# Moving one pair of heads from the float32 path to the split-float32 path in a fused attention and MLP kernel

## The chip, the cores and the metric

The kernel runs on one core of one Trainium2 chip. The metric is device time in microseconds from one launch, median of the runs shown. TensorE (PE), VectorE (DVE), ScalarE (ACT), GpSimd (POOL) and the queue of SyncE (SP), which issues nearly all loads and stores, each take their instructions in a fixed order and meet through semaphores.

## The reference

```
q, k, v: [4, 8, 768, 64] float32;  n_sink = 4, window = 128
scores = q k^T / 8, kept where key < n_sink or 0 <= query - key < window, else -1e9
a = softmax(scores);  attn = a v
x = attn as [3072, 512]
h = x @ w_in            # [3072, 2048]
out = (h * sigmoid(h)) @ w_out   # [3072, 512]
```

## The kernel before

The 3072 tokens are handled in eight chunks of 384 (half a batch each, numbered c = 0 to 7). The eight heads of a chunk are four pairs, so there are 32 pairs p = 0 to 31; pairs 0 to 3 belong to chunk 0, 4 to 7 to chunk 1, and so on. A pair's attention gives 128 columns of x. The MLP of a chunk has sixteen steps fc = 0 to 15: twelve matmuls `h<-xh,winh` and the like (line 852, 128 hidden units by 384 tokens), SiLU twice on ACT (`gh`, rounded, and `sg`, line 863 and 864), their difference `gl` on DVE (line 866), and nine matmuls into `out` (lines 878 to 880). Every MLP operand is split into a rounded high part and a remainder, so three products stand for one float32 product. The two h banks in PSUM mean that step fc + 2 cannot start on PE before ACT has read step fc.

There are two ways through attention. **The float32 way** (`f_` functions) is used for pairs p < FP: q and k are transposed on PE (line 673), the scores are full float32 matmuls (line 720, two records each in the profile), the three query blocks are masked on DVE (line 727), exponentiated on ACT (line 742), turned into a reciprocal on DVE (lines 746 and 747), normalized on ACT (line 753), transposed on PE (lines 765 to 770), copied back by ACT and DVE (lines 771 to 776), and multiplied by v in float32 (line 788). **The split way** is used for p >= FP: DVE transposes q and k (lines 390, 410), ACT and DVE split them into parts, the scores are twelve one-pass matmuls (lines 464, 468), POOL normalizes (line 505) and splits by mask (lines 536, 540), and the product with v takes six matmuls of the `o<-pq,vs` kind a head and one for the sink keys (line 591). The split way needs the sink keys of all heads laid out beforehand (`ksA`, `ksB`); the function `sinks` does that once, with four small loads into `ksn`, four small transposes into `kst` (line 300), two copies on ACT and two subtractions on DVE.

The weights come as 32 blocks of 512 KB, eight for each of four groups g (four of w_in, four of w_out). A block is loaded into `wraw` (lines 802, 805), turned into float32 bits by three DVE instructions on `wcv` (lines 41 to 43), rounded on ACT (line 826) and its remainder taken on DVE (line 828; POOL for the first six). `wraw`, `ksn` and the output staging share one tag, `ost`, with two buffers in rotation, so a load waits until the block two places before it has been converted. I write raw1_0 for block 0 of group 1, r4_0 for the reciprocals of pair 4's first head, pa0_4 for its first transposed probabilities, s5_0 for the scores of pair 5's first head, o4 for pair 4's product with v, and gh0_0 for chunk 0, step 0.

All of this is written as closures with a due time T, in units of one MLP step, and emitted in the order of T. The table `OPT` gives the due times; the framework then sets each engine's order from that, taking what is ready and earlier due. The lines that matter:

```
        at(O["tk"], sinks)
            if p < FP:
                ...
                        z = O["s1"]
                        T = O["S"] + O["F1"] + (u - 2 * HP) * z
        for g in range(NG):
            for i in range(NCC + FG):
                at(O["w"][g] + O["wd"][g] * i, lambda g=g, i=i: weight(g, i))
```

Here u = 2p + j counts heads, HP is 4, `s1` is the spacing of the float32 heads of chunk 1, `tk` the due time of `sinks`, and `w`, `wd` are the start and the spacing of a weight group.

Of the kernel before, what the change touches and what calls it, by code (L numbers as in the profile page):

```python
# [25 lines left out]

OPT = dict(
    S=7.901, s0=0.903, f_l=2.468, f_p=-1.643, f_v=3.079, f_sm=0.693, f_pt=0.795, f_av=0.251,
    tk=15.973, s1=1.65, F1=1.024, D0=2.076, w=[0.458, 8.623, 11.237, 18.573], wd=[0.85, 0.58,
    1.293, 0.67], wc=19.252, wcd=2.681, warm=7, wg=4, ord=1, edge=8, dua=15, adp=0, glp=0,  # L30
    ptv=7, fill=[0, 4, 0, 0, 1, 0, 0, 2], na=[2, 16], lod=[6, 32], nv=[0, 0], hid=[0, 0],
    ktd=[0, 0], a=dict(load=-3.44, q=0.257, k=-0.012, v=1.813, s=1.461, sd=0.613, sm=1.795,
    smd=0.605, pt0=2.725, st=3.866, pt1=3.355, av0=4.289, av1=4.669), m0=dict(act=0.108,
    m2=1.206), m=dict(act=1.068, m2=1.546), fin=0.927, FP=8,
)


# [997 lines left out]
```

## Time and profile before

| what | value |
|---|---|
| median of 2 runs | 723.79 us (722.8 to 724.79) |
| the profiled execution | 723.66 us, its span 721.8 us |
| granted TensorE clock, mean | 0.998 |
| PE busy | 705.0 us of the span |
| DVE, ACT, POOL busy | 481.3, 489.4, 281.5 us |
| loaded and stored | 61.86 MB |

Matmuls overlap in their records, so the duration of one (346 ns for a 384-wide h matmul) is about twice the step from one start to the next (0.175 us in steady state). Costs of PE work below are therefore read from start to start.

### The profile page before, as it was taken

The numbers are of one execution on the slowest core, as the hardware profiler recorded it, in microseconds if no ns is written. First come the engines' busy times: TensorE is split into PE (matmuls) and PEld (weight loads), VectorE is DVE, ScalarE is ACT, GpSimd is POOL, SyncE is SP. The second block draws the span as 40 slices with busy tenths as digits, with TensorE's granted clock in tenths as the row PEclk, the third lists the DMA queues.
The fourth block names the chain that finished last, engine by engine and source line by source line (L and its number), as shares of the span: only waits on it lengthen the run. The fifth ranks groups of instructions, "written<-read, shape, count | busy, mean of one in ns | idle before, by whom it ended". The sixth has DMA issues, their size and how long they took to land.

```text
span 721.8 us, 12275 instructions
## 1 busy us (share of the span) xinstructions
PE 705.0 (98%) x3842; PEld 624.1 (86%) x3842; DVE 481.3 (67%) x1323; ACT 489.4 (68%) x1165; POOL 281.5 (39%) x667
## 2 busy tenths in 40 slices
PE   6998999999999999999999999999999999999997
PEld 4676778798999999999999999999999999998986
DVE  5899767976776687667866777767866776731111
ACT  4889788786776777777666777777667876732112
POOL 3310000055655666444555455544554554430000
PEclk9999999999999999999999999999999999999999
DMA  7556546434522262114521353114412321001001
GB/s 180 176 154 186 148 112 173 151 84 107 147 43 40 70 187 63 22 39 138 138 41 27 84 166 66 35 34 120 136 27 41 106 58 35 1 1 45 0 1 46
DMA packets 141334, 61.86 MB, mean 86 GB/s; under 512 B 130001, under 2 KB 130001, under 8 KB 141265
## 3 DMA queue, kind: packets, MB, share of 16 engines
q1 hardware_dynamic: 140976, 61.04, 32.9%
q8 instruction: 31, 0.51, 0.3%
q14 instruction: 39, 0.31, 0.1%
q10 hardware_dynamic: 288, 0.00, 0.0%
HBM read 54.72 MB, written 6.29 MB: 85 GB/s over the span
## 4 chain that ended last, share of the span: by engine, by line
PE 81%; DMA 5%; DVE 5%; ACT 3%; POOL 2%; issue 2%; SPq 1%; DVEq 0%; POOLq 0%; ACTq 0%
PE h L852 32%; PE out L880 11%; PE out L879 11%; PE out L878 11%; PE o L575 4%; DMA wraw<-in_moe_w_in_dram 3%; PE o L788 2%; PE s L468 2%; PE s L464 2%; PE pt L520 2%; DMA wraw<-in_moe_w_out_dram 2%; PE o L591 1%; DVE wcv L43 1%; DVE wcv L42 1%; PE o L584 1%
## 5 line engine op out<-in xcount | busy, mean ns | idle before, releaser
L852 PE MATMUL h<-xh,winh 128*128 128x384 f32 x512 | 177.2, 346 | 0.0
L852 PE MATMUL h<-xh,winl 128*128 128x384 f32 x512 | 173.9, 340 | 0.0
L852 PE MATMUL h<-xl,winh 128*128 128x384 f32 x512 | 172.7, 337 | 0.0
L878 PE MATMUL out<-wouth,gh 128*128 128x512 f32 x384 | 153.2, 401 | 1.7 <-ACT gh L863 1.6
L879 PE MATMUL out<-woutl,gh 128*128 128x512 f32 x384 | 151.8, 396 | 0.5 <-DVE woutl L828 0.3
L880 PE MATMUL out<-wouth,gl 128*128 128x512 f32 x384 | 150.2, 396 | 0.0
L863 ACT ACTIVATE gh<-h 128x384 fp32r<-128x384 f32 x128 | 62.9, 492 | 104.4 <-PE h L852 100.7
L866 DVE TENSOR_TENSOR gl<-sg,gh 128x384 fp32r<-128x384 f32 x128 | 75.4, 589 | 87.2 <-ACT sg L864 84.9
L852 PEld LDWEIGHTS h<-xh,winh 128*128 128x128 f32 x512 | 96.3, 188 | 3.0 <-issue 0.9
L852 PEld LDWEIGHTS h<-xl,winh 128*128 128x128 f32 x512 | 96.5, 189 | 2.1
L852 PEld LDWEIGHTS h<-xh,winl 128*128 128x128 f32 x512 | 96.2, 188 | 0.5 <-issue 0.3
L880 PEld LDWEIGHTS out<-wouth,gl 128*128 128x128 f32 x384 | 71.8, 188 | 17.2 <-DVE gl L866 0.6
L878 PEld LDWEIGHTS out<-wouth,gh 128*128 128x128 f32 x384 | 72.2, 188 | 14.4 <-ACT gh L863 2.4
L879 PEld LDWEIGHTS out<-woutl,gh 128*128 128x128 f32 x384 | 72.1, 188 | 13.2 <-DVE woutl L828 1.3
L505 POOL TENSOR_SCALAR pm<-pm,r 128x128 f32<-128x128 f32 x144 | 61.5, 442 | 42.5 <-DVE r L490 39.2
L485 ACT ACTIVATE pm<-pm,mx 128x264 f32<-128x264 f32 (+1 forms) x144 | 70.6, 492 | 1.3 <-DVE mx L472 0.3
L440 POOL TENSOR_TENSOR vs<-vn,vs 128x256 fp32r<-128x256 f32 (+1 forms) x48 | 33.3, 695 | 91.4 <-ACT vs L438 78.2
L864 ACT ACTIVATE sg<-h 128x384 f32<-128x384 f32 x128 | 62.5, 488 | 0.5
L472 DVE CUSTOM_DVE_ANT_0 pm<-s,m 128x264 f32<-128x264 f32 (+1 forms) x144 | 52.9, 411 | 11.9 <-PE s L468 11.6
L600 DVE TENSOR_TENSOR x<-o,x 64x512 f32<-64x512 f32 x48 | 32.8, 683 | 35.5 <-ACT x L599 34.4
L419 POOL CAST ks<-ksA 128x24 fp32r<-128x24 f32 (+1 forms) x24 | 4.8, 201 | 131.7 <-PE s L468 73.0
L438 ACT CAST vs<-vn 128x256 fp32r<-128x256 f32 (+1 forms) x48 | 18.6, 388 | 50.1 <-PE o L584 49.6
(162 smaller groups left out, 1337.7 us busy)
## 6 DMA issues: line engine op xcount, KB each, us to landing
wraw<-in_moe_w_in_dram SPq DMA_DIRECT2D x16, 512.0 KB
wraw<-in_moe_w_out_dram SPq DMA_DIRECT2D x16, 512.0 KB
wchk<-in_moe_w_in_dram SPq DMA_DIRECT2D x16, 512.0 KB
wchk<-in_moe_w_out_dram SPq DMA_DIRECT2D x16, 512.0 KB
qn<-in_q_dram SPq DMA_DIRECT2D x96, 48.0 KB
kn<-in_k_dram SPq DMA_DIRECT2D x64, 64.0 KB
vn<-in_v_dram SPq DMA_DIRECT2D x32, 128.0 KB
out_dram<-ost SPq DMA_DIRECT2D x7, 512.0 KB
```

Source lines behind the costliest of these rows:

```text
L440: nc.gpsimd.tensor_tensor(vs[:, j0:, j, 1, :], vn[:, j0:, j, :], vs[:, j0:, j, 0, :], ALU.subtract)
L472: nc.vector.tensor_tensor_reduce(out=pm[:, t, off:], in0=sp[:, :w], in1=(m0, m1, m2)[min(blk, 2)], scale=-0.125, scalar=3.0e38, op0=ALU.ad ...
L485: nc.scalar.activation(x, x, AF.Exp, bias=mx[:, p, j * NTB + t : j * NTB + t + 1], scale=-1.0, accum_out=r[:, t : t + 1],)
L505: nc.gpsimd.tensor_scalar(x, x, r[:, t : t + 1], 1.0, ALU.mult, ALU.mult)
L600: nc.vector.tensor_tensor(x32[:, :n], o[0:64, :n], x32[:, :n], ALU.add)
L852: nc.tensor.matmul(hps[:, :CT], w[g][:, cc, fs], s[x], start=n == 0, stop=n == 3 * NCC - 1)
L863: nc.scalar.activation(gh, hps[:, :CT], AF.Silu)
L864: nc.scalar.activation(sg, hps[:, :CT], AF.Silu)
L866: eng.tensor_tensor(gl, sg, gh, ALU.subtract)
L878: nc.tensor.matmul(o, gh[:, ts_], wout_h[g][:, f], start=fc == 0, stop=False)
L879: nc.tensor.matmul(o, gh[:, ts_], wout_l[g][:, f], start=False, stop=False)
L880: nc.tensor.matmul(o, gl[:, ts_], wout_h[g][:, f], start=False, stop=fc == NFC - 1)
```

## The change

Only the table changes. `FP` goes from 8 to 7, so pair 7 takes the split way and three float32 pairs are left in chunk 1. `sinks` has to come before the first split pair and its due time `tk` goes from 15.973 to 7.0; `s1` goes from 1.65 to 1.225, so pairs 4 to 6 stand closer together and earlier; weight group 2 starts at 8.712 in place of 11.237, among group 1; the remaining numbers move by less.

```diff
 OPT = dict(
     S=7.901, s0=0.903, f_l=2.468, f_p=-1.643, f_v=3.079, f_sm=0.693, f_pt=0.795, f_av=0.251,
-    tk=15.973, s1=1.65, F1=1.024, D0=2.076, w=[0.458, 8.623, 11.237, 18.573], wd=[0.85, 0.58,
-    1.293, 0.67], wc=19.252, wcd=2.681, warm=7, wg=4, ord=1, edge=8, dua=15, adp=0, glp=0,
+    tk=7.0, s1=1.225, F1=1.024, D0=2.076, w=[0.557, 8.689, 8.712, 17.626], wd=[0.896, 0.616,
+    1.297, 0.665], wc=21.488, wcd=2.645, warm=7, wg=4, ord=1, edge=8, dua=15, adp=0, glp=0,
     ptv=7, fill=[0, 4, 0, 0, 1, 0, 0, 2], na=[2, 16], lod=[6, 32], nv=[0, 0], hid=[0, 0],
-    ktd=[0, 0], a=dict(load=-3.44, q=0.257, k=-0.012, v=1.813, s=1.461, sd=0.613, sm=1.795,
-    smd=0.605, pt0=2.725, st=3.866, pt1=3.355, av0=4.289, av1=4.669), m0=dict(act=0.108,
-    m2=1.206), m=dict(act=1.068, m2=1.546), fin=0.927, FP=8,
+    ktd=[0, 0], a=dict(load=-4.224, q=0.257, k=-0.072, v=1.529, s=1.461, sd=0.613, sm=1.648,
+    smd=1.248, pt0=3.067, st=4.158, pt1=3.355, av0=4.346, av1=4.938), m0=dict(act=0.108,
+    m2=1.399), m=dict(act=0.984, m2=1.546), fin=0.93, FP=7,
 )
```

What this does to the engines' orders is seen at three places. The first is the queue of loads (SP) after the last block of weight group 0; the numbers behind the names are buffer numbers. Before:

```order
L805 DMA wraw0_7_605<-in_moe_w_out_dram 128x1024
L654 DMA vn4_620<-in_v_dram 128x3x64 x2
L802 DMA wraw1_0_629<-in_moe_w_in_dram 128x1024
L802 DMA wraw1_1_646<-in_moe_w_in_dram 128x1024
L642 DMA qn5_623<-in_q_dram 128x3x64 x2
L642 DMA kn5_624<-in_k_dram 128x3x64 x2
L802 DMA wraw1_2_667<-in_moe_w_in_dram 128x1024
```

The same place in the changed program:

```order
L805 DMA wraw0_7_599<-in_moe_w_out_dram 128x1024
L654 DMA vn4_637<-in_v_dram 128x3x64 x2
L295 DMA ksn_620<-in_k_dram 8x8x64 x4
L642 DMA qn5_640<-in_q_dram 128x3x64 x2
L642 DMA kn5_641<-in_k_dram 128x3x64 x2
L802 DMA wraw1_0_646<-in_moe_w_in_dram 128x1024
L802 DMA wraw2_0_654<-in_moe_w_in_dram 128x1024
```

The sink keys' loads now stand ahead of group 1, the loads of pair 5's q and k do too, and block 0 of group 2 takes the place behind raw1_0 that raw1_1 had.

The second place is DVE around the reciprocals of pair 4's first head (r4_0: an addition, line 746, and a reciprocal, line 747). Before:

```order
L41 TENSOR_SCALAR wcv1_1_648<-wraw1_1_646 128x512
L42 SCALAR_TENSOR_TENSOR wcv1_1_648<-wraw1_1_646,wcv1_1_648 128x512
L746 TENSOR_SCALAR r4_0_688<-r4_0_688 128x3
L43 SCALAR_TENSOR_TENSOR wcv1_1_648<-wraw1_1_646,wcv1_1_648 128x512
L747 RECIPROCAL r4_0_688<-r4_0_688 128x3
```

Changed:

```order
L41 TENSOR_SCALAR wcv1_0_648<-wraw1_0_646 128x512
L746 TENSOR_SCALAR r4_0_692<-r4_0_692 128x3
L727 ISA pm4_1_739,mx_73<-s4_1_2_741,m2_96 128x264
L727 ISA mx_73 128x1
L42 SCALAR_TENSOR_TENSOR wcv1_0_648<-wraw1_0_646,wcv1_0_648 128x512
L41 TENSOR_SCALAR wcv2_0_656<-wraw2_0_654 128x512
L43 SCALAR_TENSOR_TENSOR wcv1_0_648<-wraw1_0_646,wcv1_0_648 128x512
L42 SCALAR_TENSOR_TENSOR wcv2_0_656<-wraw2_0_654,wcv2_0_656 128x512
L747 RECIPROCAL r4_0_692<-r4_0_692 128x3
```

The reciprocal stood behind work on raw1_1 and now stands behind work on raw1_0 and on raw2_0, two blocks that are loaded later in the queue above.

The third place is the first SiLU of chunk 0 on ACT and the matmuls that use it on PE. ACT before, from the normalization of pair 4's first head:

```order
L826 CAST winh1_135<-wcv1_1_648 128x512
L753 ACTIVATE pm4_0_637<-pm4_0_637,r4_0_688 128x128
L753 ACTIVATE pm4_0_637<-pm4_0_637,r4_0_688 128x256
L753 ACTIVATE pm4_0_637<-pm4_0_637,r4_0_688 128x264
L863 ACT_TABLE_LOAD
L863 ACTIVATE gh0_0_698<-h0_0_675 128x384
```

ACT in the changed program, from the last normalization of pair 4's second head:

```order
L753 ACTIVATE pm4_1_739<-pm4_1_739,r4_1_775 128x264
L771 COPY pTz0_151<-pa0_4_790 128x256
L776 COPY pTz0_151<-pb4_0_791 128x384
L826 CAST winh1_135<-wcv1_1_673 128x512
L742 ACTIVATE pm5_0_817,r5_0_882<-pm5_0_817,mx_73 128x128
L863 ACT_TABLE_LOAD
L863 ACTIVATE gh0_0_734<-h0_0_709 128x384
```

PE ahead of the first use of gh0_0 in the changed program; before, the first two of these rows (the scores s5_0) stood directly ahead of it:

```order
L720 MATMUL s5_0_0_818<-kT5_687,qdf_149 128x128
L720 MATMUL s5_0_0_818<-kT5_687,qdf_149 128x256
L720 MATMUL s5_0_2_819<-kT5_687,qdf_149 128x264
L788 MATMUL o4_838<-pTz0_151,vn4_637 64x384
L788 MATMUL o4_838<-pTz0_151,vn4_637 64x256
L788 MATMUL o4_838<-pTz0_151,vn4_637 64x128
L673 MATMUL qt6_850<-ident_58,qn6_756 128x128 x3
L673 MATMUL kt6_851<-ident_58,kn6_757 128x128 x2
L878 MATMUL out0_0_826<-wouth0_133,gh0_0_734 128x512
```

The SiLU came right after pair 4's first normalization and now comes after the second one, after the copies of pa0_4 and after the rounding of raw1_1; on PE a product with v and pair 6's transposes have moved ahead of the MLP.

## The prediction

> **What bounds the kernel now.** I begin with the busy times and the chain that ended last.
>
> ```profile
> PE 705.0 (98%) x3842; PEld 624.1 (86%) x3842; DVE 481.3 (67%) x1323; ACT 489.4 (68%) x1165; POOL 281.5 (39%) x667
> PE 81%; DMA 5%; DVE 5%; ACT 3%; POOL 2%; issue 2%; SPq 1%; DVEq 0%; POOLq 0%; ACTq 0%
> ```
>
> PE is the bound on average: 98% busy, 81% of the chain. The 67% and 68% of DVE and ACT are averages over stages, so I look at stretches next (columns: length; busy time of PE, PEld, DVE, ACT, POOL with instruction counts; granted clock; DMA share; GB/s).
>
> ```profile
> 50.00:60.00 10.00, 8.79 (x47) 6.61 (x46) 9.54 (x32) 8.90 (x20) 0.00 (x0) 1.00 0.89 220
> 200.00:210.00 10.00, 10.00 (x58) 9.19 (x58) 7.72 (x15) 6.22 (x14) 7.35 (x15) 1.00 0.29 47
> ```
>
> From 200 us on PE has no gap and less PE work is less time. Between 50 and 60 us it is otherwise: DVE is busy for 9.54 of 10, ACT for 8.90, the DMA engines for 0.89, POOL does nothing, and PE is the one that waits. This is where pairs 4 and 5 of chunk 1, the conversion of weight group 1 and the first MLP steps meet, and where the change moves most. The waits of PE name the partners (total, times, longest, in us).
>
> ```profile
> PE out L878 <- ACT gh L863: 1.6, 2, 1.1
> PE pa L765 <- ACT pm L753: 0.6, 1, 0.6
> ```
>
> So there are two prices: the work that PE loses, which is worth its full length, and the waits around 50 to 70 us, which the new order can shorten or lengthen.
>
> **Term 1: the PE work that goes.** A float32 head, from the start of one group to the start of the next; then a pair's transposes of q and k:
>
> ```profile
> 38.11 0.33 PE L765 MATMUL pa<-ident,pm 128*128 128x128 f32 x1
> 38.82 1.27 PE L720 MATMUL s<-kT,qdf 128*128 128x128 f32 x6
> 39.92 1.05 PE L695 MATMUL f<-m,ident 128*128 128x264 f32 x4
> 40.90 1.51 PE L788 MATMUL o<-pTz,vn 128*64 128x384 f32 x6
> 42.34 0.33 PE L765 MATMUL pa<-ident,pm 128*128 128x128 f32 x1
> 21.27 0.55 PE L673 MATMUL qt<-ident,qn 128*128 128x128 f32 x3
> 21.99 0.27 PE L765 MATMUL pa<-ident,pm 128*128 128x128 f32 x1
> ```
>
> Transposes 0.71, scores 1.10, product with v 1.44, and 0.72 a pair ahead of them: 2 x 3.25 + 0.72 = 7.22 us. A split head of a first half, as pair 7 is one, in the undisturbed middle of the run:
>
> ```profile
> 335.14 0.22 PE L464 MATMUL s<-ks,qd 128*128 128x128 f32 x1
> 335.86 0.40 PE L878 MATMUL out<-wouth,gh 128*128 128x512 f32 x1
> 342.86 0.49 PE L520 MATMUL pt<-ident,pm 128*128 128x128 f32 x3
> 343.11 0.42 PE L852 MATMUL h<-xh,winh 128*128 128x384 f32 x1
> 349.82 0.63 PE L575 MATMUL o<-pq,vs 128*128 128x256 f32 x4
> 350.53 0.39 PE L878 MATMUL out<-wouth,gh 128*128 128x512 f32 x1
> ```
>
> Scores 0.72, transposes 0.25, product 0.71: 2 x 1.68 = 3.36 us. **Term 1 is 3.36 - 7.22 = -3.9 us.** The DVE, ACT and POOL work of a split pair is hidden in this middle, where PE has no gap beside it, and pair 7 comes after the crowded stretch; I cost it at nothing. With that cover gone one wait on POOL before a sink product would be paid, at most some 0.7 us. `sinks` itself is not new, it moves.
>
> **Term 2: the waits between 47 and 70 us.** PE's order is the same up to 47.41. Then I follow the four orders through the new program, each engine starting an instruction when it is free and its partner done, with durations of before. The loads first (queue of SP, issue times):
>
> ```profile
> 43.45 3.84 SPq L802 DMA_DIRECT2D wraw<-in_moe_w_in_dram  x2
> 47.93 1.58 SPq L642 DMA_DIRECT2D qn<-in_q_dram  x2
> 49.61 0.96 SPq L642 DMA_DIRECT2D kn<-in_k_dram  x2
> 47.89 0.41 DVE L41 TENSOR_SCALAR wcv<-wraw 128x512 int32<-128x512 int32 x1
> 48.33 0.69 DVE L42 SCALAR_TENSOR_TENSOR wcv<-wraw,wcv 128x512 int32<-128x512 int32 x1
> 54.38 0.17 DVE L747 RECIPROCAL r<-r 128x3 f32<-128x3 f32 x1
> ```
>
> Before, raw1_0 left at 43.45 and DVE began on it at 47.89: 4.4 us. Pair 5's q waited until 47.93 in the queue, since its buffer is free only when PE has transposed pair 4's q. In the new queue the sink keys take the buffer that raw1_0 had at 43.45, and raw1_0 stands behind that waiting q. On PE pair 4's transposes now come behind four h matmuls and o3: 47.41 + 0.7 + 1.44 = 49.6. So q and k of pair 5 leave from 49.9 to 51.9, raw1_0 at 51.9 in place of 43.45, raw2_0 at 52.4 (it needs the sink keys' buffer, which four small transposes on PE free at about 52). With 4.4 us each they land at 56.3 and 56.8.
>
> Every 0.41 + 0.69 + 0.69 of conversion takes about 1.75 from start to start. DVE must do lines 41 of raw2_0, 43 of raw1_0 and 42 of raw2_0 before the reciprocal r4_0: 56.8 + 0.4 + 0.6 + 0.6 = 58.4, against 54.38. ACT and PE follow:
>
> ```profile
> 54.80 0.62 ACT L826 CAST winh<-wcv 128x512 fp32r<-128x512 f32 x1
> 55.32 1.21 ACT L753 ACTIVATE pm<-pm,r 128x128 f32<-128x128 f32 x3
> 56.54 1.28 ACT L863 ACT_TABLE_LOAD   x1
> 57.84 0.49 ACT L863 ACTIVATE gh<-h 128x384 fp32r<-128x384 f32 x1
> 58.74 0.56 DVE L866 TENSOR_TENSOR gl<-sg,gh 128x384 fp32r<-128x384 f32 x1
> 55.77 0.33 PE L765 MATMUL pa<-ident,pm 128*128 128x128 f32 x1 [0.61 <-ACT pm L753]
> 58.38 0.50 PE L878 MATMUL out<-wouth,gh 128*128 128x512 f32 x1 [0.46 <-ACT gh L863]
> 59.89 0.85 PE L880 MATMUL out<-wouth,gl 128*128 128x512 f32 x3
> 60.58 0.34 PE L852 MATMUL h<-xh,winh 128*128 128x384 f32 x1
> ```
>
> Normalization 58.6 to 59.8, so pa0_4 starts near 59.1, not 55.77, while PE has finished s4_1 at about 55.5 (s4_0, the 0.72 of pair 5's transposes, s4_1). That is a gap of some 3.6 us, and nothing in PE's order fills it: the next MLP step needs an h bank, which gh0_0 frees. gh0_0 in turn stands on ACT behind the rounding of raw1_1. That block's buffer is raw1_0's, free at 57.8; it lands at 62.2, is converted by 64.0, rounded by 64.6; then one exponential (a third of the 1.21, 0.4), the table load and gh0_0 end at 66.8, against 58.33. The `gl` that follows stands on DVE behind line 41 of raw2_1, whose buffer is raw1_1's, free at 64.0: lands at 68.4, gl0_0 ends at 69.4, the last three matmuls take 0.7, and h0_2 starts at 70.1 in place of 60.58.
>
> Of these 9.5 us PE has used 2.9 for work that came later before: o4 (1.44), pair 6's transposes (0.72), the rest of s5_0 (0.45 by width out of the 1.10), the sink transposes (0.3, an estimate). **Term 2 is 9.5 - 2.9 = +6.6 us.** Three weight loads stand in series in it, so their length sets its bounds. The chain shows the fastest and the slowest:
>
> ```profile
> 58.30 3.53 DMA wraw<-in_moe_w_out_dram
> 8.02 5.19 DMA wraw<-in_moe_w_in_dram
> ```
>
> At 3.5 us each it is 6.6 - 2.7 = 3.9, at 5.2 us each 6.6 + 2.4 = 9.0. I keep 4.4, the row nearest in place. The other bound is 0: if the planner's order fits what really lands, DVE is never held and PE waits no more than before.
>
> **Term 3: what comes back.** Of the later waits of before (the second of the two on gh, one on `woutl`, about 2 us together), some must go, since group 2 is loaded earlier and the float32 pairs end earlier; as many new ones of the same kind (SiLU behind a rounding, `gl` behind a conversion) stand in the orders until pair 6 is through. Bounds +3 and -3; I take -1.0, as the weights of groups 2 and 3 run ahead of their use.
>
> **Sum.** The profiled execution took 723.66 us (span 721.8), 0.13 below the median. 723.66 - 3.9 + 6.6 - 1.0 = **725.4 us**.
>
> **The rivals.** *The saving arrives whole.* Terms 2 and 3 are nothing or cancel: 723.66 - 3.9 = 719.8, within 718.5 to 722. For it: after 200 us PE has no gap, so 3.9 us cannot be lost there, and a wait that only moves from one engine to the next costs nothing. Against it: the first term needs a crowded stretch to absorb more attention work than before without a cost. It decides for this if raw1_0 is converted by about 53 us. Chance 0.30.
>
> *The gap puts the clock down.* The trace has one such event:
>
> ```profile
> 5.00:8.50 3.50, 1.09 (x8) 1.00 1.04 223
> 8.50:12.00 3.50, 3.50 (x11) 0.51 0.94 293
> ```
>
> PE was busy for 1.09 of 3.5 us, and the granted clock of the next 3.5 us was 0.51. Term 2 makes a gap of about 3.6 us near 56 to 59 us. If a stretch of that length falls into it, the 3.4 us of PE work behind run at half speed, 1.7 us more, and with the slow end of the loads (9.0 in place of 6.6): 725.4 + 1.7 + 2.4 = 729.5, within 727.5 to 732. This ends clearly slower than before. [...] Chance 0.17. [...]
>
> *The pair does not leave the float32 path, or the sink keys come too late.* The orders show pair 7's scores on lines 464 and 468 and `kst` far ahead of them; 0.01.
>
> **How the numbers follow.** Forecast case (PE is held near 55 to 70 us, 722 to 727.5): 0.52. With 0.30 and 0.17 of the rivals, the range that leaves out no more than 2 in 10 is 719.3 to 730: it holds nearly all of the first rival and the lower half of the second. A measurement of this kernel can tell 2% from no change, that is 14.5 us; none of the cases goes so far. Term 1 and all waits of PE after 40 us together are less than 14.5 us, so faster by 2% has 0.01; slower would need more than twice term 2: 0.02.
>
> **What would show it.** Right: raw1_0 leaves near 52 us; DVE idles before lines 41 of raw1_0 and raw2_0, ended by a DMA; r4_0 at about 58; PE waits 3 us or more ahead of pa0_4 and 1 to 2 us ahead of gh0_0's first use; h0_2 starts near 70; from 200 us on every step stands at one constant distance from before. Wrong: if h0_2 starts before 65, loads land faster or SP is not held, and the first rival is true; if the granted clock shows a second 0.5 near 60 us, the second. Pair 7 is costed wrong if PE waits for POOL or ACT between 120 and 165 us by more than 1 us.

## The result, and the profile after

| | before | changed |
|---|---|---|
| median (2 runs) | 723.79 us (722.8 to 724.79) | 731.32 us (731.0 to 731.63) |
| ratio to before | | 1.0104, 95% interval 1.0082 to 1.0125 |
| profiled execution, its span | 723.66, 721.8 us | 731.63, 729.9 us |
| mean granted clock | 0.998 | 0.992 |

The change costs 7.5 us; the prediction was 725.4 in a range up to 730.0. The changed kernel's page, busy times and chain:

```profile
PE 703.8 (96%) x3832; PEld 623.2 (85%) x3832; DVE 489.6 (67%) x1333; ACT 487.2 (67%) x1162; POOL 298.5 (41%) x695
PE 87%; DVE 4%; DMA 4%; ACT 1%; SPq 1%; issue 1%; POOL 1%; DVEq 0%; ACTq 0%
```

PE has ten records fewer, DVE 8.3 us and POOL 17 us more work. In stretches (columns as in the prediction): the two that the prediction shows of before, 50 to 60 and 200 to 210 us, now in the changed kernel, and between them the gap and its sequel in steps of 3.41 us:

```profile
50.00:60.00 10.00, 6.44 (x38) 4.63 (x36) 5.05 (x22) 6.78 (x21) 0.00 (x0) 0.96 0.75 191
55.86:59.27 3.41, 0.74 (x3) 0.30 (x2) 2.17 (x10) 3.02 (x11) 0.00 (x0) 1.00 1.05 288
59.27:62.68 3.41, 1.00 (x4) 0.67 (x5) 3.09 (x8) 2.05 (x5) 0.00 (x0) 0.50 0.51 109
62.68:66.09 3.41, 3.23 (x11) 1.83 (x9) 2.25 (x5) 2.14 (x6) 0.00 (x0) 0.50 0.79 245
200.00:210.00 10.00, 10.00 (x57) 9.06 (x56) 6.63 (x22) 8.51 (x23) 6.73 (x18) 1.00 0.17 56
```

Between 50 and 60 us PE is busy for 6.44 of 10 us where it was busy for 8.79 before, and from 59.27 on it runs at clock 0.50 for 6.8 us. After 200 us nothing is lost: the first h matmul of chunk 2 starts at 242.65 in place of 234.80, that of chunk 3 at 326.36 in place of 318.37, a distance of 7.9 and 8.0 us. The waits of PE (total, times, longest):

```profile
PE pa L765 <- ACT pm L753: 5.1, 1, 5.1
PE pt L520 <- POOL pm L505: 1.6, 3, 0.7
PE s L720 <- DVE mx L727: 1.5, 1, 1.5
PE s L720 <- ACT pTz L776: 1.4, 2, 1.2
PE kt L673 <- DVE mx L727: 1.4, 2, 1.2
```

One wait of 5.1 us ahead of pa0_4, three of 1.2 to 1.5 us that were not there, and three shorter ones on POOL. Timeline of PE (start, length, wait in brackets), of SP's queue and of DVE in the changed kernel:

```profile
55.12 1.48 PE L720 MATMUL s<-kT,qlf 128*128 128x128 f32 x6
61.68 0.48 PE L765 MATMUL pa<-ident,pm 128*128 128x128 f32 x1 [5.08 <-ACT pm L753]
69.44 0.48 PE L878 MATMUL out<-wouth,gh 128*128 128x512 f32 x1
72.28 0.34 PE L852 MATMUL h<-xh,winh 128*128 128x384 f32 x1
84.98 0.68 PE L720 MATMUL s<-kT,qlf 128*128 128x264 f32 x2 [1.49 <-DVE mx L727]
96.91 0.92 PE L720 MATMUL s<-kT,qlf 128*128 128x128 f32 x4 [1.19 <-ACT pTz L776]
```

```profile
43.60 1.37 SPq L295 DMA_DIRECT2D ksn<-in_k_dram  x4
50.72 0.92 SPq L642 DMA_DIRECT2D qn<-in_q_dram  x2
52.81 1.38 SPq L802 DMA_DIRECT2D wraw<-in_moe_w_in_dram  x2
59.42 0.43 DVE L41 TENSOR_SCALAR wcv<-wraw 128x512 int32<-128x512 int32 x1 [0.55 <-DMA wraw<-in_moe_w_in_dram]
60.96 0.17 DVE L747 RECIPROCAL r<-r 128x3 f32<-128x3 f32 x1
```

The chain of term 2 is there link by link: sink keys, waiting q of pair 5, raw1_0 at 52.81, raw2_0 that DVE waits for, r4_0 at 60.96, pa0_4 at 61.68, h0_2 at 72.28.

To compare runs I use one number: from the trace, each matmul's distance to the next start, less the median distance of its kind (its line and shape) in the trace of before, is what PE **loses** there. A loss is a wait or a matmul that ran slow. Without loss, the matmuls of before take 692.66 us and those with FP=7 take 689.08. The losses in us by stretch, with the medians of the runs (2 for before and after, 4 to 9 otherwise) and ratios to before on the same chip (before was 723.7 to 724.3 there):

```
run                          45-75  75-120  120-175   rest   median  ratio, 95%
before                         4.3     2.2      3.1   12.6   723.8
changed                       11.6     4.9      4.3   12.7   731.3   1.0104 (1.0082-1.0125)
1  FP=7 alone                  4.4     2.8     17.5   13.3   735.7   1.0165 (1.0151-1.0179)
2  sinks early alone          11.7     1.5      2.5   12.3   729.8   1.0085 (1.0071-1.0099)
3  changed, sinks late         6.0     4.9      8.4   13.5   730.8   1.0103 (1.0085-1.0120)
4  changed, gap filled         6.7     6.7      8.2   13.1   738.0   1.0204 (1.0190-1.0218)
5  sinks early, raw1_0 first   9.1     4.9      4.1   13.0   732.0   1.0100 (1.0076-1.0124)
6  changed, old weights       11.9     1.7     12.4   13.2   737.4   1.0187 (1.0170-1.0204)
7  changed, old stages        11.7     5.1      7.4   13.5   735.7   1.0152 (1.0132-1.0173)
8  FP=7, new stages            4.3     4.2     16.8   12.4   736.7   1.0175 (1.0158-1.0192)
9  changed, own buffer        11.5     6.5      8.3   15.1   740.8   1.0235 (1.0215-1.0255)
10 before, less PE in pair 7   4.4     2.5      4.4   12.5   722.4   0.9967 (0.9954-0.9980)
11 changed, less DVE          11.7     8.1      5.1   13.4   736.9   1.0175 (1.0158-1.0191)
12 before, less DVE            7.5     5.7      2.7   12.6   729.0   1.0061 (1.0047-1.0076)
13 before, no group 3          4.4     1.8      1.9   12.5   722.0   0.9979 (0.9969-0.9989)
14 FP=7, no group 3            4.4     2.8      1.8   12.5   720.1   0.9950 (0.9933-0.9966)
15 FP=7, pair 7 later          4.4     2.8     19.2   13.0   737.8   1.0190 (1.0173-1.0207)
16 FP=7, stream earlier        4.3     5.9     13.6   12.6   735.4   1.0163 (1.0146-1.0180)
17 FP=7, pair 7 earlier        4.4     4.4     12.1   12.3   731.8   1.0109 (1.0094-1.0124)
18 as 17, stream earlier       4.4     6.7      8.7   12.6   730.8   1.0100 (1.0082-1.0118)
```

From before to changed: -3.6 of work, +7.3, +2.7 and +1.2 of losses, +0.1 in the rest, and 0.4 behind the last matmul: 723.66 + 8.1 = 731.8, against 731.63 profiled.

### The profile page after: what moved, and what is told of

Read it like the earlier page. It is cut to its first block, busy times and chain, and to the rows that moved or that the text cites. A ratio compares the mean times of both kernels' runs of the same rounds, so it can differ in the third digit from the quotient of the medians.

```text
span 729.9 us, 12314 instructions
## 1 busy us (share of the span) xinstructions
PE 703.8 (96%) x3832; PEld 623.2 (85%) x3832; DVE 489.6 (67%) x1333; ACT 487.2 (67%) x1162; POOL 298.5 (41%) x695
## 4 chain that ended last, share of the span: by engine, by line
PE 87%; DVE 4%; DMA 4%; ACT 1%; SPq 1%; issue 1%; POOL 1%; DVEq 0%; ACTq 0%
PE h L852 35%; PE out L880 12%; PE out L879 12%; PE out L878 12%; PE o L575 4%; DMA wraw<-in_moe_w_in_dram 3%; PE s L468 2%; PE s L464 2%; PE o L788 2%; PE pt L520 2%; PE o L591 1%; PE o L584 1%; DMA wraw<-in_moe_w_out_dram 1%; DVE wcv L42 1%; DVE wcv L43 1%
## 5 line engine op out<-in xcount | busy, mean ns | idle before, releaser
L505 POOL TENSOR_SCALAR pm<-pm,r 128x128 f32<-128x128 f32 x150 | 64.7, 448 | 42.9 <-DVE r L490 33.4
L485 ACT ACTIVATE pm<-pm,mx 128x264 f32<-128x264 f32 (+1 forms) x150 | 73.5, 492 | 3.7 <-DVE mx L472 2.9
L440 POOL TENSOR_TENSOR vs<-vn,vs 128x256 fp32r<-128x256 f32 (+1 forms) x50 | 36.0, 721 | 94.5 <-ACT vs L438 78.2
L472 DVE CUSTOM_DVE_ANT_0 pm<-s,m 128x264 f32<-128x264 f32 (+1 forms) x150 | 54.9, 410 | 11.4 <-PE s L468 11.3
L600 DVE TENSOR_TENSOR x<-o,x 64x512 f32<-64x512 f32 (+1 forms) x50 | 33.9, 678 | 36.9 <-ACT x L599 35.7
L540 POOL TENSOR_SCALAR_AFFINE_SELECT pq<-pq 128x384 fp32r<-128x384 f32 (+1 forms) x100 | 52.3, 523 | 6.4
```

Of the source, the lines that this page charges most:

```text
L440: nc.gpsimd.tensor_tensor(vs[:, j0:, j, 1, :], vn[:, j0:, j, :], vs[:, j0:, j, 0, :], ALU.subtract)
L472: nc.vector.tensor_tensor_reduce(out=pm[:, t, off:], in0=sp[:, :w], in1=(m0, m1, m2)[min(blk, 2)], scale=-0.125, scalar=3.0e38, op0=ALU.ad ...
L485: nc.scalar.activation(x, x, AF.Exp, bias=mx[:, p, j * NTB + t : j * NTB + t + 1], scale=-1.0, accum_out=r[:, t : t + 1],)
L505: nc.gpsimd.tensor_scalar(x, x, r[:, t : t + 1], 1.0, ALU.mult, ALU.mult)
L540: nc.gpsimd.affine_select(out=own, in_=own, pattern=[[0, n], [1, P]], compare_op=ALU.is_ge, fill=0.0, base=0, channel_multiplier=-1,)
```

## The experiments: the early sink keys

**1. FP=7 alone.**

```diff
-    tk=15.973, ... FP=8,
+    tk=15.973, ... FP=7,
```

> The kernel before with FP=7 alone; sinks stays at 15.973 and every other number stands as before. Theory (the early sink keys cost the time, not the pair): raw1_0 leaves at about 43.5 us as before, PE waits under 1 us ahead of pa0_4, no half clock near 60 us, and the PE work of the pair, -3.6 to -3.9 us, arrives less up to 1.5 us of POOL waits in pair 7: 720 to 722 us. Rival A (the split pair itself upsets the middle: its DVE and POOL work delays conversions and SiLU): waits between 80 and 165 us grow by as much as is saved or more, 723.5 to 728. Rival B (the sink keys come too late for pair 7, PE waits for them in front of its sink scores): one wait of 1 us or more on kst or ksA between 120 and 150 us, 722 to 725.

735.71 us: all three missed the time. Up to 120 us it goes as before, as the theory says; rival A named the place, but not the size: pair 7's passage loses 17.5 us in place of 3.1. The section on pair 7 follows it.

**2. The early sink keys alone.**

```diff
-    tk=15.973,
+    tk=7.0,
```

> The kernel before with tk=7.0 alone: sinks is early, FP stays 8, weights and spacing as before. Theory (the early sink keys hold raw1_0 behind pair 5's waiting q and k): raw1_0 leaves at 50 to 52 us, r4_0 comes at 57 us or later, PE waits 3 to 5 us ahead of pa0_4; 723.8 + 4 to 7 = 728 to 731 us, with a half clock near 60 us if the gap covers a whole window. Rival (group 2 among group 1, not the sink keys, holds DVE: here raw1_1 follows raw1_0 as before): r4_0 by 56, a wait of at most 2 us, 723.5 to 725.5.

729.77 us, +5.8: the theory. Queue of SP and the wait of PE in this run:

```profile
48.08 0.92 SPq L642 DMA_DIRECT2D qn<-in_q_dram  x2
50.17 2.91 SPq L802 DMA_DIRECT2D wraw<-in_moe_w_in_dram  x2
PE pa L765 <- ACT pm L753: 4.4, 1, 4.4
```

From 60 to 80 us the mean clock was 0.74, so the half clock came; that a gap has to cover a whole window for it, no run shows. Group 2 stands where it stood before, so the gap does not need it. 45 to 75 us lose 7.4 us more, and 1.3 of it comes back later.

**3. The changed kernel with late sink keys.**

```diff
-    tk=7.0,
+    tk=15.973,
```

> The changed kernel with tk back at 15.973 alone: FP=7, the new weight and spacing numbers stay. Theory (the early sink keys): raw1_0 leaves at about 43.5 us, no wait of 3 us ahead of pa0_4, no half clock near 60 us; the 6.4 us that 50 to 70 us lost go, less what group 2 among group 1 still holds back (0 to 2): 725 to 727 us. Rival A (group 2 among group 1 is the cause): the wait stays over 3 us, 729.5 to 732. Rival B (the waits of 80 to 100 and 130 to 160 us follow from the late stretch, not from a cause of their own): they go too, 720 to 723.

730.84 us, above the theory's 727. The early loss falls by 5.6 us and no half clock stands near 60 us (1.00 on the mean from 40 to 60 and from 60 to 80 us), as the theory says, but 4.1 us come back behind 120 us, with waits on POOL line 505 (3.5 us in place of 1.6) and a half clock (0.82 and 0.61 on the mean from 137 to 140 and from 140 to 143 us). The time lies in rival A's range without its wait. So the early sink keys cause the early loss, and yet taking them back hardly helps the whole.

**4. The gap filled.**

```diff
-    fill=[0, 4, 0, 0, 1, 0, 0, 2],
+    fill=[0, 4, 0, 0, 1, 0, 0, 2, 0, 9],
```

> The changed kernel with nine 264-wide float32 matmuls without a use put behind s4_1 on PE, into the gap ahead of pa0_4 (0.49 us each by the two records of such a matmul, 4.4 us of the 5.1). Theory (the half clock behind the gap costs time by itself): the granted clock stays 1.0 from 55 to 70 us, the 4.4 us of PE work that ran at half speed between 61.7 and 66.1 take 2.2 us less: 728.5 to 730 us. Rival (the loads of raw1_1 and the conversions set gh0_0 and h0_2 whatever the clock is): the clock stays 1.0 and h0_2 still starts near 72: 731 to 732 us. If the clock still falls to 0.5, the gap was not its cause.

The clock stays at 1.0 from 55 to 70 us, so the gap made the half clock. But PE used gh0_0 no earlier (at 69.58, in the changed kernel at 69.44): at full speed it waits for DVE's `mx` and then for gh instead. PE in run 4:

```profile
65.82 0.68 PE L720 MATMUL s<-kT,qdf 128*128 128x264 f32 x2 [1.81 <-DVE mx L727]
69.58 0.50 PE L878 MATMUL out<-wouth,gh 128*128 128x512 f32 x1 [0.68 <-ACT gh L863]
71.08 0.34 PE L852 MATMUL h<-xh,winh 128*128 128x384 f32 x1
```

h0_2 starts at 71.08 in place of 72.28, but mainly because in this order its first six matmuls stand ahead of the three `gl` matmuls of step 0. Where both programs have done the same work, ahead of the next transposes of probabilities (line 765), run 4 is at 74.03 and the changed kernel at 74.39. So the half clock was worth 0.4 us there, not 2.2: the rival. The total, 738.0, lies above the rival's range and is not a price of the clock: the filler moved later orders too, and pair 7 lost 3.9 us more.

**5. raw1_0 ahead of the waiting q and k.**

```diff
-    tk=15.973, ... w=[0.458, 8.623, 11.237, 18.573],
+    tk=7.0, ... w=[0.458, 8.1, 11.237, 18.573],
```

> The kernel before with tk=7.0 as in the run with sinks early alone, and group 1 of the weights due from 8.1 in place of 8.623, so that raw1_0 stands ahead of pair 5's q and k again, behind the sink keys alone. Theory (raw1_0 is late because it stands behind loads that wait for pair 4's transposes): raw1_0 leaves when block 7 of group 0 frees its buffer, at about 47 us as raw1_1 did before (46.95), in place of 50.17; r4_0 at 54 to 56, the wait ahead of pa0_4 falls from 4.4 to 2 or less, no half clock: 724 to 726.5 us. Rival (the sink keys take one of the two buffers, so every block of group 1 is one place later whatever the queue): gh0_0 stays late by 5 us or more, 727.5 to 730.

raw1_0 left at 47.25, as expected, and the wait ahead of pa0_4 fell to 0.8 us. But raw1_1 left at 52.88 in place of 46.95, PE used gh0_0 first at 63.26 in place of 58.38, then waited 2.0 us for gh0_1. SP's queue in this run:

```profile
47.25 0.36 SPq L802 DMA_DIRECT2D wraw<-in_moe_w_in_dram  x1
52.88 0.35 SPq L802 DMA_DIRECT2D wraw<-in_moe_w_in_dram  x1
```

That is the rival's mechanism: raw1_1 waited for the sink keys' buffer, which the last of their transposes freed at 52.85. Of the 7.4 us that 45 to 75 us lost more in run 2, 4.8 stayed with the queue mended. The time, 732.0, lies above the rival's 730: 75 to 175 us lost 5.0 us more than in run 2, and why is open.

**9. A buffer of their own for the sink keys.**

```diff
-            ksn = p1.tile([B * NS, H, D], F32, tag="ost", name="ksn", bufs=2)
+            ksn = p1.tile([B * NS, H, D], F32, tag="ksn", name="ksn", bufs=1)
```

> The changed kernel with the sink keys' tile ksn in a tag of its own in place of ost, so that it no longer takes one of the two buffers through which the weight blocks rotate; the table stays. Theory (the sink keys cost because they hold a buffer and the queue ahead of raw1_0): raw1_0 leaves by about 43.5 us, the wait ahead of pa0_4 is under 1 us and there is no half clock near 60 us. If nothing takes the 6.4 us back, 724.5 to 726 us. Rival (the stretch from 50 to 150 us is paced by the weight stream and DVE, and gives the time back as waits ahead of pair 7's transposes, as in the run with late sink keys): waits of 120 to 170 us grow from 4.3 to 8 us or more, 728 to 732 us.

740.8 us, the slowest, above both ranges. With nothing left to hold them, the sinks' loads went out among group 0's (SP's queue in this run):

```profile
25.58 0.38 SPq L295 DMA_DIRECT2D ksn<-in_k_dram  x1
28.39 0.68 SPq L382 DMA_DIRECT2D vsn<-in_v_dram  x2
48.76 3.49 SPq L802 DMA_DIRECT2D wraw<-in_moe_w_in_dram  x2
```

Group 0's last block left at 46.06 in place of 39.68 and raw1_0 at 48.76. So this run does not isolate the buffer; what is known of its price rests on run 5.

## The experiments: pair 7

In run 1, PE in pair 7's passage, and its clock:

```profile
134.65 1.02 PE L520 MATMUL pt<-ident,pm 128*128 128x128 f32 x3 [1.40 <-POOL pm L505]
136.83 1.54 PE L575 MATMUL o<-pq,vs 128*128 128x256 f32 x6 [1.16 <-DVE pq L531]
141.04 0.69 PE L852 MATMUL h<-xh,winh 128*128 128x384 f32 x1 [1.26 <-ACT winh L826]
...
132.45:135.86 3.41, 1.53 (x5) 0.58 (x5) 1.92 (x5) 0.84 (x3) 2.62 (x9) 1.00 0.19 42
135.86:139.27 3.41, 2.44 (x9) 2.13 (x9) 3.05 (x5) 2.33 (x5) 3.26 (x7) 0.50 0.21 34
139.27:142.69 3.42, 2.16 (x6) 1.14 (x4) 3.39 (x7) 0.62 (x1) 2.50 (x4) 0.50 0.37 109
142.69:146.10 3.41, 2.72 (x11) 2.36 (x10) 3.00 (x5) 2.13 (x3) 0.48 (x3) 0.50 0.83 227
146.10:149.51 3.41, 2.73 (x7) 2.44 (x8) 2.75 (x5) 2.41 (x7) 1.32 (x2) 0.50 0.13 19
149.51:152.92 3.41, 3.41 (x10) 2.82 (x10) 2.77 (x5) 1.38 (x3) 1.67 (x2) 0.50 0.26 80
```

PE waits in turn for POOL's normalization, DVE's remainder and ACT's rounding of a weight, none over 1.4 us, and then works at half clock for 17 us. Of the 17.5 us some 9.5 stand ahead of matmuls that waited and 8.0 at matmuls that ran slow.

**6 and 7. The changed kernel with before's weight numbers, and with before's stage table.**

```diff
-    w=[0.557, 8.689, 8.712, 17.626], wd=[0.896, 0.616, 1.297, 0.665], wc=21.488, wcd=2.645,
+    w=[0.458, 8.623, 11.237, 18.573], wd=[0.85, 0.58, 1.293, 0.67], wc=19.252, wcd=2.681,
```

```diff
-    a=dict(load=-4.224, ..., smd=1.248, pt0=3.067, ...), m0=dict(..., m2=1.399), m=dict(act=0.984, ...), fin=0.93,
+    a=dict(load=-3.44, ..., smd=0.605, pt0=2.725, ...), m0=dict(..., m2=1.206), m=dict(act=1.068, ...), fin=0.927,
```

> The changed kernel with before's weight numbers w, wd, wc, wcd: sinks stays early, group 2 starts at 11.237 again. Theory (the early sink keys make the gap, group 2 among group 1 adds little to it): the wait ahead of pa0_4 stays at 4 to 5 us as with the sinks early alone (4.4); what group 2 gained later is gone, and pair 7 meets its conversions as in the run of FP=7 alone, 5 us or more between 120 and 165 us: 731 to 736. Rival (group 2 among group 1 is what holds DVE and ACT): the wait ahead of pa0_4 falls under 3 us and the waits of 80 to 100 us go, 725 to 728.

> The changed kernel with before's table a of the split pairs and before's m0, m and fin (the transposes of the probabilities due at 2.725 after the pair's start in place of 3.067, and so on). Theory (pair 7 has no cover behind its scores, so the distance from its exponentials to its transposes decides what PE waits there): waits on POOL line 505 and 558 between 125 and 165 us grow from 2.4 us to 4 to 8, with a half clock near 140: 733 to 738. Rival (the stages play no part, the waits come from the weights): 730.5 to 732.

737.4 and 735.7 us. Run 6 is the theory, 1.4 us above its range. It prices the new weight numbers, all of them together: with the old ones 75 to 120 us lose 1.7 in place of 4.9, and pair 7 loses 12.4 in place of 4.3. Up to 100 us the changed kernel converts blocks of groups 1 and 2 alone (group 3's first is rounded at 117.5), and its two long waits of that stretch, 1.49 and 1.19 us, stand before 97 us; so there the early group 2 is the likely part. Run 7 lies in the theory's range, but not by its waits: those on POOL did not grow, and PE waited 2.4 us for a `gh` that stood on ACT behind work of pair 7 which itself waited for POOL. It prices the new stages, with `m0`, `m` and `fin`: 3.1 us at pair 7. Both sets of numbers buy pair 7's passage, the first at a cost of 3.2 us earlier.

**8. FP=7 alone with the new stage table** (the `a` of run 7 the other way round, on run 1).

> The kernel before with FP=7 and the new table a of the split pairs; sinks late, weights and spacing of before. Theory (pair 7's stages stand too close together in the run of FP=7 alone, 735.7): the waits on POOL line 505 fall by half, the half clock from 136 to 153 us shortens, 726 to 731. Rival (the conversions of group 2 are late beside pair 7's own work on DVE): the waits on winh and wouth and the half clock stay, 733 to 737. If pair 7 then costs nothing, 720 to 722.

736.7 us, the rival: the stage table alone, without the other new numbers, helps nothing.

**10. Before, with less PE work in pair 7.**

```diff
-            for kb, x0, q0 in (...):
+            for kb, x0, q0 in (...)[: 1 if p == 7 else 3]:
-            for t, (sp, keys, mask) in enumerate(todo):
+            for t, (sp, keys, mask) in enumerate(todo[: 2 if p == 7 else 3]):
```

> The kernel before, float32 pair 7 kept, with part of its PE work left out and its work on the other engines kept: the third score matmul of each head (264 of 648 columns of 1.10 us, 0.45), the second and third matmul of each product (384 of 768 columns of 1.44, 0.72), and two transposes of k (0.24): 2 x 1.17 + 0.24 = 2.6 us. Theory of the prediction's first term (PE work in pair 7's place is worth its full length): 723.9 - 2.6 = 721.3, within 720.5 to 722. Rival (up to 150 us the weight stream sets when PE gets its MLP steps, so PE work taken out there turns into waiting): the waits of PE between 110 and 165 us grow by about as much, 723 to 724.5.

Two of k's transposes are left out too (not shown). 722.38 against 724.33: -1.9 us (the ratio's interval gives 1.4 to 3.3), of 2.6 taken away. The time lies between theory and rival: PE work in this place is worth more than half of its length, perhaps all of it. The saving is real; something that comes with the split way eats it.

**13 and 14. No weight group 3, without and with pair 7 on the split way.** MLP steps 12 to 15 take group 2's weights. The edit of run 13; run 14 has FP=7 as well:

```diff
-            g, f = divmod(fc, FG)
+            g, f = divmod(fc, FG); g = min(g, 2)
-                at(O["w"][g] + O["wd"][g] * i, lambda g=g, i=i: weight(g, i))
+                at(O["w"][g] + O["wd"][g] * i, lambda g=g, i=i: weight(g, i) if g < 3 else None)
```

> The kernel before with weight group 3 neither loaded nor converted: MLP steps 12 to 15 take group 2's weights in its place, with the same matmuls. It is the control of the run of FP=7 alone with the same left out: the weight stream ends near 118 us in place of 143, and DVE has 8 x 2.5 = 20 us less to do between 110 and 145. The losses of before between 110 and 175 us are about 3.4 us, so at most that can go: 721 to 724.

> The kernel before with FP=7 alone, and weight group 3 neither loaded nor converted (MLP steps 12 to 15 take group 2's weights). Theory (pair 7's split way collides with the conversions of the last weight group, in the orders of DVE and ACT; by itself it is cheap): the losses of 120 to 175 us fall from 17.5 us to 5 or less and no half clock is left; against its control the time is -3.6 to -1, so 718 to 722. Rival (the pair's own chain from scores over POOL to the product has no cover, with or without the weights): losses stay over 10 us there, and the time is 6 us or more above the control, 728 to 734.

722.03 and 720.07 us. Here the split pair pays: -2.0 us against its control, where with group 3 it cost 11.8. Its passage loses 1.8 us (1.9 in the control) in place of 17.5, and PE is full (run 14, then run 1):

```profile
130.00:140.00 10.00, 10.00 (x58) 9.13 (x57) 6.94 (x15) 8.41 (x19) 6.51 (x19) 1.00 0.28 46
...
130.00:140.00 10.00, 6.49 (x22) 3.78 (x20) 7.43 (x18) 5.24 (x17) 8.11 (x21) 0.79 0.38 93
```

So the dear thing is the meeting of pair 7's split way with the last weight group. Two roads lead from the group to PE: its conversions stand between pair 7's stages on DVE and ACT, and MLP steps 12 to 15, which PE could do meanwhile, wait for its blocks. The last block is rounded at 143 us before, at 150 in the changed kernel and at 160 in run 1.

**15 and 16. Pair 7 later, and group 3 earlier**, both on run 1.

```diff
+            T += 1.2 if p == 7 else 0.0
```

```diff
-    w=[0.458, 8.623, 11.237, 18.573],
+    w=[0.458, 8.623, 11.237, 17.0],
```

> The kernel before with FP=7 alone and pair 7's due times 1.2 steps later (about 6 us), towards the end of the weight stream. Theory (the collision with the last conversions is the cost): losses of 120 to 175 us fall from 17.5 to 5 to 12 us, 725 to 731. Rival (no cover for its chain, wherever it stands): 734 to 738; chunk 1's first MLP step could also come to wait for pair 7, which would show as a wait of h on x.

> The kernel before with FP=7 alone and weight group 3 due from 17.0 in place of 18.573 (about 8 us earlier). Theory (collision with the last conversions): the last block is rounded before 155 us in place of 160 and pair 7 loses less, 727 to 732. Rival (DVE is full there whichever comes first): 734 to 738.

737.8 and 735.4 us, the rivals both times. (In run 15 pair 8's sink values are split before pair 7's second product, which then takes them in place of its own.) In run 16 the last block is rounded at 149 us in place of 160, and pair 7 still loses 13.6. What the two have in common shows in the program's order: PE goes from pair 7's scores straight to its transposes. It has no cover there, no MLP work that it could do while DVE, ACT and POOL turn the scores into probabilities. Counting the MLP matmuls that stand on PE between the second head's scores and its transposes, beside the loss of 120 to 175 us:

```
run                 14    18    chg   11    7     17    6     4     9     3     1     8     15    16
MLP matmuls         40    37    33    33    26    25    18    12    12    11    7     0     0     0
loss, us            1.8   8.7   4.3   5.1   7.4   12.1  12.4  8.2   8.3   8.4   17.5  16.8  19.2  13.6
```

**17 and 18. More cover for pair 7.** Run 1 with due times of its own for pair 7, and then group 3 from 17.6 as well:

```diff
-            A = O["a"]
+            A = dict(O["a"], **(dict(load=-4.4, q=-0.5, k=-0.7, v=1.0, s=0.6, sd=0.6, sm=0.9, smd=1.0,
+                pt0=3.067, st=4.158, pt1=3.6, av0=4.4, av1=5.0) if p == 7 else {}))
```

> The kernel before with FP=7 alone and due times of its own for pair 7: scores due 0.86 steps earlier, the second head's exponentials 0.9 - 1.3 steps earlier, transposes, sink keys and products 0.1 to 0.35 later, so its stages stand further apart. In the program's order 25 MLP matmuls stand on PE between the second head's scores and its transposes, 24 of them between the transposes of the two heads, in place of 7 and 0 with FP=7 alone. Theory (what counts is how much MLP work PE has behind the scores while ACT, DVE and POOL bring the probabilities): the losses of 120 to 175 us fall from 17.5 us to 6 to 9, as with the changed kernel and before's stage table (26 matmuls, 7.4 us): 724 to 728. Rival (DVE's conversions set it, whatever stands on PE): 733 to 737.

> As the run with pair 7's own due times, and weight group 3 due from 17.6 in place of 18.573: 37 MLP matmuls stand between the second head's scores and its transposes, 21 of them between the two heads' transposes (33 and 21 in the changed kernel, which lost 4.3 us there; 40 and 21 without group 3, 1.8 us). Theory (cover): losses of 120 to 175 us of 2 to 5 us; the stretch from 45 to 75 us stays as before: 720 to 723.5, the first version under before. Rival (DVE's conversions): 730 or more.

731.8 and 730.8 us: run 17 between theory and rival, run 18 in the rival's range, with a loss of 8.7 us where the theory gave 2 to 5. With every conversion kept, the new due times take 5.4 and 8.8 of the 17.5 us away. That speaks for cover as one cause, but does not isolate it, since the same due times also move pair 7's work on DVE, ACT and POOL against the conversions. The rest of the loss stays, and run 18 loses 3.9 us more than run 1 between 75 and 120 us. How the rest divides between DVE's order and ACT's is open, and no version that does all the work beats before.

## The experiments: taking work off DVE

**11 and 12. Fourteen remainders on POOL, in the changed kernel and in before.**

```diff
-    lod=[6, 32],
+    lod=[20, 32],
```

> The changed kernel with the remainders (line 828) of weight blocks 6 to 19 on POOL in place of DVE: 14 x 0.685 = 9.6 us of DVE work less between 45 and 115 us, where POOL is nearly idle; a remainder takes 1.27 us on POOL in place of 0.69. Theory (conversions on DVE pace the stretch): the waits of 80 to 100 us go and the last weight block is rounded 2 us or more before its 150 us: 727 to 730. Rival (the loads and the two buffers pace it, not DVE's own work): 730.5 to 732.5.

> The kernel before with the remainders (line 828) of weight blocks 6 to 19 on POOL in place of DVE, the control of the run on the changed kernel. Theory (before has little waiting left between 70 and 160 us, 4.9 us in all, so DVE relieved gives little): 722.5 to 724.5. Rival (DVE paces before as much as after): 719 to 722.

736.9 and 729.0 us, against all four expectations: run 12 is 4.7 us above before, run 11 12.6 us above it where the changed kernel is 7.5. Groups of DVE between 45 and 110 us (busy, mean ns), in before and then in run 12, and two rows of run 12's timeline:

```profile
L42 DVE SCALAR_TENSOR_TENSOR wcv<-wraw,wcv 128x512 int32<-128x512 int32 x16 | 10.9, 683 | 0.2
L866 DVE TENSOR_TENSOR gl<-sg,gh 128x384 fp32r<-128x384 f32 x9 | 5.0, 554 | 2.2 <-ACT sg L864 1.3 <-PE out L880 0.8
...
L42 DVE SCALAR_TENSOR_TENSOR wcv<-wraw,wcv 128x512 int32<-128x512 int32 x14 | 12.4, 885 | 0.2
L866 DVE TENSOR_TENSOR gl<-sg,gh 128x384 fp32r<-128x384 f32 x7 | 6.0, 863 | 5.1 <-PE out L880 1.8 <-ACT sg L864 1.7 <-POOL winl L828 1.6
...
60.76 1.28 POOL L828 TENSOR_TENSOR winl<-wcv,winh 128x512 fp32r<-128x512 f32 x1 [2.69 <-ACT winh L826]
61.18 1.28 DVE L866 TENSOR_TENSOR gl<-sg,gh 128x384 fp32r<-128x384 f32 x1 [0.59 <-ACT sg L864]
```

The `gl` that starts while POOL works takes 1.28 us in place of 0.55 and ends 0.42 after POOL has. Over 45 to 110 us DVE's instructions grew by about 8.5 us in each run (each against the lower tenth of its kind in before), of the 9.6 that were taken away. Why the time rose, and did not merely stay, is not isolated; in run 12 the last block was rounded at 151 us in place of 143. The two rows show one longer `gl` beside POOL's work; by what the one holds up the other, no run shows.

## Why the prediction was wrong, point by point

**Term 1, the PE work that goes (-3.9): right.** The matmuls without loss take 3.6 us less, and run 10 found 1.9 of 2.6 us at pair 7's place in the time.

**Pair 7's DVE, ACT and POOL work (nothing, or 0.7 with the cover gone): the step that was furthest off, hidden in the total.** It was costed from the middle of the run, where PE is full. Alone (run 1) pair 7's passage loses 14.4 us more than before; without the last weight group (run 14) no more than its control. In the changed kernel it shows as only +1.2 us, three waits on POOL of 0.4 to 0.7 and one of 0.8 on the sink product, because the new weight and stage numbers spare it the rest (runs 6 and 7). The sign that the prediction set for this, over 1 us of waits on POOL or ACT between 120 and 165 us, is there, 2.4 us in all. That "pair 7 comes after the crowded stretch" was wrong: group 3 is converted there.

**Term 2, the waits of 47 to 70 us (+6.6, bounds 0 to 9.0): right, measured +7.3.** Predicted and measured: raw1_0 leaves 51.9 and 52.81; raw2_0 lands 56.8 and 59.42; r4_0 58.4 and 60.96; pa0_4 59.1 and 61.68, its wait 3.6 and 5.08; gh0_0 ends 66.8 and 69.29; h0_2 70.1 and 72.28. The 2.2 us at the end come from raw2_0: it left at 53.85 in place of 52.4, and DVE began on it 5.6 us later in place of 4.4, while the DMA engines were full (1.05). The sink transposes, put at 0.3 us without a source, took 0.36 (52.37 to 52.73). Run 2 gives the sink keys alone as the cause, at 5.8 us of the time; the buffer that they hold counts for more there than the waiting queue (run 5).

**Term 3, what comes back later (-1.0, bounds +3 and -3): the step that failed in the sum.** 75 to 120 us lost 2.7 us more: +2.7 in place of -1.0, within the bounds, but of the wrong sign. That is 3.7 of the 6.2 us by which the forecast was low; pair 7's 1.2, another 0.7 in term 2 and 0.3 in term 1 make most of the rest. Term 3 rested on "the weights of groups 2 and 3 run ahead of their use"; the last block came 7 us later than before. Nor were the new waits of the kind it named, MLP steps behind weights: the 1.49 and 1.19 us are score matmuls of float32 pairs that wait for DVE's mask and for ACT's copy. Run 6 shows that the new weight numbers make the loss.

**The rivals.** The saving did not arrive whole. The clock went down where the second rival said, for two stretches (59.27 to 66.09), but together with the forecast case, not instead of it. The measured time lies in this rival's range (727.5 to 732) by luck: its clock cost 0.4 us (run 4), not 1.7, and the sum was filled by term 3 and pair 7, which it did not have. Its condition was met only in part: the gap, 56.60 to 61.68, was longer than a stretch of 3.41 us, but covered none of them whole, and PE was busy for 0.74 and 1.00 us in the two that it touched. The distance after 200 us was constant, as said.

## What to carry to other kernels

An edit that saves work on the bound engine and adds it to others is to be costed where it stands, not where the same work was seen to be hidden: the same pair cost 11.8 us of the time with the last weights in conversion and saved 2.0 without. Ask how much of its own work the bound engine has in its order behind the new chain's first step. And ask what a moved load holds, not only what it stands ahead of: four small loads in a two-buffer rotation made a weight group start 6.7 us later (run 2: raw1_0 from 43.45 to 50.17).

## What the runs showed of the hardware that was not expected

**The clock falls without a wholly idle stretch.** In before the half clock that began at 8.56 us lasted 3.41 us (to 11.97), in the changed kernel the one at 59.27 lasted 6.82 (to 66.09), in run 1 the one at 135.86 lasted 17.06 (to 152.92): one, two and five times 3.41. So in the traces that show a half clock between 30 and 690 us I laid stretches of 3.41 us in step with it, from 15 us on, and took PE's busy share. At full clock, all 21 stretches ahead of a half-clock one were busy for 0.00 to 0.54; the lowest shares that were not followed by one are 0.53 (four times) and 0.56. At half clock, the 19 stretches followed by another were busy for 0.17 to 0.82, the 21 followed by full clock for 0.83 to 1.00. In run 1 above, the half clock came behind a stretch with 1.53 of 3.41, went on behind 2.44, 2.16, 2.72 and 2.73 of 3.41, and ended behind 3.41. So in run 1 it came with waits of at most 1.4 us, close together, and in no run did the full clock return before PE had been busy for 0.83 of a stretch.

**POOL was no free place for DVE's work** (runs 11 and 12): about 8.5 of 9.6 us came back as longer DVE instructions.
